# First batch of an attention and ReGLU kernel rebuilt: loads on 128 partitions, 64x64 transposes, one array tiling, operations picked by priority

## The chip, the cores and the metric

The kernel runs on one core of a Trainium2 chip. The metric is device time in microseconds (us), lower is better. "Fast" runs agree within about 1.5%; a run far above is "slow" and is left out of comparisons. Ratios are the mean time of one kernel's fast runs over the mean of the other's fast runs of the same rounds, so they are not quite the ratio of the medians that are quoted.

TensorE (PE) multiplies. Here it works as one 128x128 array (one matmul of 192 columns every 82 ns in the kernel before) or in 64x64 tiles, four of which run together; part of batch 0 ran in 128x64 tiles before. VectorE (DVE) and ScalarE (ACT) take results out of PSUM here. GpSimd (POOL) issues the loads, which cast float32 to bfloat16 on the way: 48.76 MB were read from HBM and 24.38 MB written by their queue. So the GB/s of the profile count the bytes written to the core's memory.

## The reference

```python
q, k, v: (8, 12, 448, 64)            # batch, heads, tokens, head size
scores = q @ k.T / sqrt(64)
attn   = maximum(scores, 0) ** 2 / 448
x      = (attn @ v) transposed to (3584, 768)
gate, val = maximum(x @ w_gate, 0), x @ w_val     # (768, 1536) each
out    = (gate * val) @ w_out                     # (1536, 768)
```

A batch is 448 tokens. Batch 0 has a schedule of its own, since nothing can be overlapped with its loads; later batches interleave the attention of one batch with the feed-forward part (FFN) of the batch before.

## The kernel before

A planner in Python gives every operation a start time from assumed durations and load rates, and the instructions are emitted in that order. TensorE ran strictly in it: matched by the name of what they write, none of the 8,414 matmuls of the kernel before starts more than 4 places from its place in the program. Batch 0 is split into two groups of its token columns, 192 and 256, so that the FFN of the first group can start early.

```python
def PARTS(b):
    return [(0, 192), (192, S - 192)] if b == 0 else [(0, S)]
...
# transposes: one head's q on partitions 0-63, its k on 64-127, 14 matmuls of 128 columns a head pair
nc.tensor.transpose(t_ps[64 * h2:64 * h2 + 64, i * 128:(i + 1) * 128],
                    st.qk[:, 4 * g + 2 * j + h2, t, :], ident)
...
class Product:                       # one output tile of 128 rows of the FFN
    def piece(self, row, k):
        if row is None:              # whole array: ONE matmul for 128 rows of the sum
            nc.tensor.matmul(self.out(), lhsT=self.weights(p, k), rhs=self.moving(p, k), ...)
            return
        p = slice(64 * row, 64 * row + 64)
        for col in range(2):         # 64x64 tiles: FOUR matmuls for the same work (2 rows x 2 columns)
            c = slice(64 * col, 64 * col + 64)
            ins = nc.tensor.matmul(self.out()[c], lhsT=self.weights(p, k)[:, c], rhs=self.moving(p, k), ...)
...
def chain_ops(prods):  ...           # 64x64: upper and lower half of the sum run staggered
def full_ops(prods):   ...           # 128x128
...
# batch 0 on the whole array, the rest in 64x64 tiles
ffn = full_ops([x for x in prods if x.b == 0]) + chain_ops([x for x in prods if x.b > 0])
```

Each matmul comes with a load of its weights, so a piece is 2 TensorE instructions on the whole array and 8 in 64x64 tiles. On the whole array a piece takes about columns/2400 us (82 ns were measured at 192 columns, 109 at 256), and four 64x64 matmuls side by side take the same.

Of the kernel before, what the change touches and what calls it, by code (L numbers as in the profile page):

```python
# [47 lines left out]
class Planner:  # L48
    LAT = 0.26
    NOUT = 8  # L50
    SWITCH = 0.095

# [37 lines left out]
    def commit(self, op, s, e):  # L90
        op.start, op.eng = s, e
# [25 lines left out]
def plan(att, ffn, others, pool, nburst, calm):  # L117
# [3 lines left out]
    P = Planner()  # L121
    ai = fi = pi = 0
# [4 lines left out]
    while ai < len(att) or fi < len(ffn) or pend or pi < len(pool):  # L127
# [12 lines left out]
        A = P.best(att[ai][0]) if ai < len(att) else None  # L140
        F = P.best(ffn[fi][1]) if fi < len(ffn) else None
        pick = None
        if A is not None and F is not None:
            if att[ai][1] == last_burst:
                pick = "A" if A[0] <= F[0] + 0.3 else "F"
            elif since >= gap:
                pick = "A" if A[0] <= F[0] + 0.1 else "F"
            else:
                pick = "F" if F[0] <= A[0] + 0.1 else "A"
        elif A is not None:  # L150
            pick = "A"
        elif F is not None:
            pick = "F"
        if pick == "A":
            cands.append((A[0], 2, A[2], 2, "PE", att[ai][0]))
# [7 lines left out]
        elif kind == 1:  # L163
            pend.remove(op)
        elif pick == "A":
# [22 lines left out]
def kernel(  # L188
# [100 lines left out]


    def PARTS(b):
        return [(0, 192), (192, S - 192)] if b == 0 else [(0, S)]
# [6 lines left out]
    def load_heads(b, h0, n, what="kv"):  # L299
        if b not in bat:  # L300
            bat[b] = Batch()
            bat[b].buf = Buf(r_in, NT if b >= XBAR_FROM else HP)
# [11 lines left out]
        rows = lambda x: x[b, hs].rearrange("h (p t) d -> p h t d", t=NT)  # L314
        rate = (240.0 if h0 == 4 else 290.0) if b == 0 else 340.0
        if "k" in what:
            k_op = dma_in(lambda: tile_of("qk", NT)[64:128, hs], rows(k), 64 * n, 112 * n, rate=rate, alloc=[st.buf] if h0 == 0 else [])
            q_op = dma_in(lambda: tile_of("qk", NT)[0:64, hs], rows(q), 64 * n, 112 * n, rate=rate)
            for h in range(h0, h0 + n):
                st.qk_op[h] = (k_op, q_op)  # L320
        if "v" in what:
            v0 = dma_in(lambda: tile_of("vv", NC + 2)[0:64, hs, 1:NC + 2], rows(v)[:, :, 0:NC + 1], 64 * n, 64 * n,
                        alloc=[st.vbuf] if h0 == 0 else [], rate=340.0)
            v1 = dma_in(lambda: tile_of("vv", NC + 2)[64:128, hs, 0:NC + 1], rows(v)[:, :, NC:NT], 64 * n, 64 * n, rate=340.0)
            for h in range(h0, h0 + n):
                st.v_op[h] = (v0, v1)
# [3 lines left out]
    def slot_order(b):  # L330
        return SIG if b % 2 == 0 else [SIG[-1]] + SIG[:-1]

# [7 lines left out]
    def columns_of(b):  # L340
        st = bat[b]
        if not hasattr(st, "qkT"):
            st.qkT = tpool.tile([128, 2, HP, S], BF16, name="qkT")
# [12 lines left out]
    def idle(n):  # L356
        for _ in range(n):
            nc.tensor.matmul(bank("w_ps"), lhsT=zeros[:, :128], rhs=zeros, start=True, stop=True)

    def transpose_pair(b, g, j):  # L360
# [3 lines left out]
        box = {}  # L364

        def emit():
            t_ps = box["t"] = bank("t_ps", BF16)
            for i, t in enumerate(slot_order(b)):
                for h2 in range(2):
                    nc.tensor.transpose(t_ps[64 * h2:64 * h2 + 64, i * 128:(i + 1) * 128],  # L370
                                        st.qk[:, 4 * g + 2 * j + h2, t, :], ident)

        def emit_copy():
            dst = columns_of(b)[:, :, 2 * g + j, :].rearrange("p a (t c) -> p t a c", c=P2)
            src = box["t"][:, :2 * S].rearrange("p (t a c) -> p t a c", t=NT, a=2)
            if cp.eng == "ACT":
                nc.scalar.copy(dst, src)
            else:
                nc.vector.tensor_copy(dst, src)  # L379

        h = 4 * g + 2 * j
        op = Op({"PE": 0.5 if g or b else 0.95}, emit, mode="C", deps=list(st.qk_op[h]) + list(st.qk_op[h + 1]) + [id_op],
                alloc=[ps], reads=[st.buf])
# [586 lines left out]
```

## Time and profile before

| | before |
|---|---|
| time | 434.10 us, median of 4 runs, one of 726 us included (the three others: 431.43 to 435.44, median 432.75) |
| span of the profiled run | 431.6 us |
| products alone, columns/2400 summed over the trace | 385.3 us |
| products done from 20 to 70 us, by the same sum | 36.6 us |
| TensorE instructions | 16,828 |

The first lines are of the page of the kernel before. The rows of digits show the busy share in 40 slices of the span (9 is 90% or more), PEclk the granted clock in tenths. "q8" is a DMA queue of kind "instruction": packets, MB and share of the DMA engines. The last line is the summary of the chain of waits.

```profile
span 431.6 us, 18155 instructions
PE 418.6 (97%) x8414; PEld 364.2 (84%) x8414; DVE 185.5 (43%) x346; ACT 241.8 (56%) x363; POOL 46.3 (11%) x72
PE   6699999999999999999999999999999999999995
PEclk9689999999999999999999999999999999999999
DMA  7999999894089946948865993790003200040014
q8 instruction: 66, 1.08, 1.0%
PE 92%; DMA 4%; POOL 1%; issue 0%; ACT 0%; SPq 0%; DVE 0%; POOLq 0%
```

TensorE is the limit. The DMA engines are full until about 70 us, and later only in some stretches.

The stretches from 25 to 70 us of the same run: busy time of each engine in the stretch with the number of its instructions, then clock, DMA share and GB/s.

```profile
core 0: us, PE busy (x) PEld busy (x) DVE busy (x) ACT busy (x) POOL busy (x), PEclk, DMA share, GB/s
25.00:40.00 15.00, 14.98 (x238) 11.36 (x235) 11.66 (x23) 12.05 (x23) 6.87 (x10) 1.00 1.40 199
40.00:55.00 15.00, 15.00 (x166) 10.86 (x164) 9.05 (x20) 10.59 (x17) 5.74 (x8) 1.00 1.39 201
55.00:70.00 15.00, 15.00 (x184) 10.53 (x183) 7.99 (x17) 9.44 (x17) 1.49 (x2) 1.00 1.30 203
```

TensorE never waits there (588 matmuls in 45 us). What it loses there is mostly extra time at changes of tiling. Three lines of the timeline, with start and duration in us:

```profile
37.11 0.67 PE L632 MATMUL g_ps<-xT,wg 128*128 128x192 bf16 x6
37.70 0.38 PE L494 MATMUL s_ps<-qkT 64*64 64x448 bf16 x4
38.02 0.67 PE L632 MATMUL v_ps<-xT,wv 128*128 128x192 bf16 x6
```

Matmuls of 192 columns follow each other every 82 ns, but the first one after a change of tiling ends 189 ns after the one before it. There are 70 such changes from 25 to 100 us, 7.9 us in all.

### The profile page before, as it was taken

The page shows a single profiled execution, that of the slowest core. Times are in us where ns is not written, and L with a number is a line of the kernel's source. Part 1 is how long each engine was busy: PE and PEld are TensorE (multiplying, and loading weights), DVE is VectorE, ACT ScalarE, POOL GpSimd, SP SyncE. Part 2 cuts the span into 40 slices and gives each one's busy share as a digit, 9 for nine tenths or more (in the row PEclk, how much of TensorE's full clock was granted, in tenths as well). Part 3 has the DMA queues.
Part 4 walks back from the last instruction along what each step waited for, and adds up shares of the span by engine and source line. Part 5 has one row for each costly group of instructions (what it writes and reads, how often), then busy time and mean ns, then how long its engine had stood idle before and what let it go on. Part 6 is the DMA issues. An engine that isn't in the chain of part 4 may idle for free.

```text
span 431.6 us, 18155 instructions
## 1 busy us (share of the span) xinstructions
PE 418.6 (97%) x8414; PEld 364.2 (84%) x8414; DVE 185.5 (43%) x346; ACT 241.8 (56%) x363; POOL 46.3 (11%) x72
## 2 busy tenths in 40 slices
PE   6699999999999999999999999999999999999995
PEld 2477776566688999899998999999998999999984
DVE  3776645224741665444435436533434434102200
ACT  2487666445766876664547656774547645332221
POOL 8536210010002002000200110010000000000000
PEclk9689999999999999999999999999999999999999
DMA  7999999894089946948865993790003200040014
GB/s 100 192 198 199 202 203 176 129 162 80 12 122 171 183 66 71 192 119 116 128 93 100 168 175 43 103 185 32 3 3 77 76 2 4 3 112 3 4 44 107
DMA packets 75213, 44.83 MB, mean 104 GB/s; under 512 B 34560, under 2 KB 71680, under 8 KB 75136
## 3 DMA queue, kind: packets, MB, share of 16 engines
q0 software_dynamic: 37856, 24.38, 39.8%
q1 hardware_dynamic: 37200, 19.17, 24.1%
q8 instruction: 66, 1.08, 1.0%
q10 hardware_dynamic: 80, 0.10, 0.1%
q14 instruction: 11, 0.09, 0.1%
HBM read 48.76 MB, written 11.01 MB: 138 GB/s over the span
## 4 chain that ended last, share of the span: by engine, by line
PE 92%; DMA 4%; POOL 1%; issue 0%; ACT 0%; SPq 0%; DVE 0%; POOLq 0%
PE o_ps L642 23%; PE v_ps L642 22%; PE g_ps L642 22%; PE s_ps L494 7%; PE s_ps L550 6%; PE v_ps L632 4%; PE g_ps L632 3%; DMA qkT<-spare 2%; PE o_ps L632 2%; DMA qk<-in_q_dram 2%; PE s_ps L501 1%; PE x_ps L575 1%; PE t_ps L370 1%; POOL qk L265 1%; POOL vv L265 0%
## 5 line engine op out<-in xcount | busy, mean ns | idle before, releaser
L511 ACT ACTIVATE r_sb<-s_ps 128x896 bf16<-128x896 f32 (+4 forms) x169 | 150.2, 895 | 73.4 <-PE s_ps L494 58.8
L642 PE MATMUL g_ps<-xT,wg 64*64 64x448 bf16 x2016 | 183.6, 349 | 0.3 <-ACT xT L596 0.3
L642 PE MATMUL v_ps<-xT,wv 64*64 64x448 bf16 x2016 | 176.5, 349 | 0.0
L529 DVE TENSOR_TENSOR at<-r_sb 128x896 bf16<-128x896 bf16 (+4 forms) x163 | 99.7, 616 | 99.8 <-ACT r_sb L511 99.6
L642 PE MATMUL o_ps<-wo,hT 64*64 64x384 bf16 x2400 | 126.0, 323 | 0.4 <-issue 0.4
L642 PEld LDWEIGHTS <-wg 64*64 64x64 bf16 x2016 | 113.1, 107 | 5.4 <-issue 0.5
L642 PEld LDWEIGHTS <-wv 64*64 64x64 bf16 x2016 | 113.0, 107 | 5.3
L642 PEld LDWEIGHTS <-hT 64*64 64x64 bf16 x2400 | 101.4, 107 | 12.1 <-issue 1.2
L732 DVE TENSOR_TENSOR hT<-v_ps,g_sb 128x448 bf16<-128x448 f32 (+2 forms) x108 | 61.8, 572 | 111.8 <-PE v_ps L642 97.9
L725 ACT ACTIVATE g_sb<-g_ps 128x448 bf16<-128x448 f32 (+2 forms) x107 | 53.7, 502 | 57.8 <-PE g_ps L642 46.7
L494 PE MATMUL s_ps<-qkT 64*64 64x448 bf16 (+2 forms) x648 | 66.8, 341 | 2.4 <-DVE qkT L379 1.1
L777 ACT ACTIVATE o_sb<-o_ps 128x384 f32<-128x384 f32 (+1 forms) x55 | 27.2, 494 | 31.1 <-PE o_ps L642 22.5
L494 PEld LDWEIGHTS <-qkT 64*64 64x64 bf16 x648 | 30.9, 109 | 10.9 <-issue 6.1
L550 PE MATMUL s_ps<-at,vv 64*64 64x448 bf16 x588 | 39.6, 350 | 0.0
L596 ACT CAST xT<-s_ps 128x896 bf16<-128x896 f32 (+1 forms) x22 | 19.6, 892 | 20.6 <-PE s_ps L550 20.0
L550 PEld LDWEIGHTS <-vv 64*64 64x64 bf16 x612 | 26.8, 108 | 4.2 <-issue 1.8
L265 POOL DMA_DIRECT2D vv<-in_v_dram x22 | 15.5, 717 | 42.5 <-PE s_ps L550 32.8
L847 POOL COPY mark<-qkT 64x1 bf16<-64x1 bf16 x5 | 1.0, 198 | 175.8 <-DMA qkT<-spare 175.8
L632 PE MATMUL v_ps<-xT,wv 128*128 128x192 bf16 (+1 forms) x144 | 17.9, 261 | 0.0
L632 PE MATMUL g_ps<-xT,wg 128*128 128x192 bf16 (+1 forms) x144 | 17.8, 260 | 0.0
L632 PEld LDWEIGHTS <-wv 128*128 128x128 bf16 x144 | 11.6, 98 | 4.7 <-issue 4.0
L632 PEld LDWEIGHTS <-wg 128*128 128x128 bf16 x144 | 12.9, 98 | 1.5 <-issue 0.6
(36 smaller groups left out, 134.0 us busy)
## 6 DMA issues: line engine op xcount, KB each, us to landing
out_dram<-o_sb SPq DMA_DIRECT2D x54, 192.0 KB, 3.2
vv<-in_v_dram POOLq DMA_DIRECT2D x12, 384.0 KB, 12.5
qk<-in_k_dram POOLq DMA_DIRECT2D x6, 672.0 KB, 7.3
qk<-in_q_dram POOLq DMA_DIRECT2D x6, 672.0 KB, 10.8
wg<-in_moe_w_gate_dram POOLq DMA_DIRECT2D x6, 384.0 KB, 11.2
wv<-in_moe_w_val_dram POOLq DMA_DIRECT2D x6, 384.0 KB, 11.4
wo<-in_moe_w_out_dram POOLq DMA_DIRECT2D x2, 1152.0 KB, 17.2
qk<-in_k_dram POOLq DMA_DIRECT2D x5, 224.0 KB, 10.6
```

The source lines that it names most:

```text
L265: op = Op({"POOL": 0.58 + 0.0004 * n_desc}, lambda: nc.gpsimd.dma_start(out=dst(), in_=src), deps=deps, alloc=alloc, xfer=kb / rate)
L370: nc.tensor.transpose(t_ps[64 * h2:64 * h2 + 64, i * 128:(i + 1) * 128], st.qk[:, 4 * g + 2 * j + h2, t, :], ident)
L494: nc.tensor.matmul(half_of(h2)[o:o + P2, m * n:(m + 1) * n], lhsT=kq(1, j, h2, key_off(b) + c * 128 + o, P2), rhs=kq(0, j, h2, self.c0, n) ...
L511: nc.scalar.activation(dst, src, AF.Relu)
L529: lambda: nc.vector.tensor_tensor(self.at_tile(i), loc["r"][:, :2 * ne], loc["r"][:, :2 * ne], ALU.mult),
L550: ins = nc.tensor.matmul(x_of(slice(64 * h2, 64 * h2 + 64), j), lhsT=st.vv[p, 4 * g + 2 * j + h2, (NC + 1) * (1 - row) if tail else 1 + c, :],
L596: nc.scalar.copy(dst, src)
L632: nc.tensor.matmul(self.out(), lhsT=self.weights(p, k), rhs=self.moving(p, k), start=(k == 0), stop=(k == self.nk - 1))
L642: ins = nc.tensor.matmul(self.out()[c], lhsT=self.weights(p, k)[:, c], rhs=self.moving(p, k), start=(row == 0 and k == 0), stop=(row == 1 ...
L725: nc.scalar.activation(loc["gs"], gp.out(), AF.Relu)
L732: nc.vector.tensor_tensor(hs["hT"][:, mf, t0:t0 + n], vp.out(), loc["gs"], ALU.mult)
L777: nc.scalar.activation(out=dst, in_=src, func=AF.Copy, scale=float(out_scale))
```

## The change

Its intent: batch 0 no longer changes the tiling, the loads of keys and queries of batches 0 and 1 reach all partitions, and the head of the kernel takes whatever is ready. In core, with cuts marked:

```diff
 def PARTS(b):
-    return [(0, 192), (192, S - 192)] if b == 0 else [(0, S)]
+    return [((NT - QA) * P2, QA * P2), (0, (NT - QA) * P2)] if b == 0 else [(0, S)]     # QA = 3: again 192 and 256
 ...
 # loads of batches 0 and 1: two heads side by side on 128 partitions, queries of batch 0 in two pieces (a, b)
+    pt = lambda x: x[b, hs].rearrange("(a c) (p t) d -> (c p) a t d", c=2, t=NT)
+    LOADS = ("k0002 a0002 k0404 a0404 I k0202 a0804 a0202 v0004 k0804 b0012 v0408 g0 g1 g2 kqv1004 g3 "
+             "kqv1804 kqv1404 g4 g5 o0 o1")
 ...
 # transposes: 28 matmuls of 64 columns a head pair, in the two diagonal 64x64 tiles
+    nc.tensor.transpose(t_ps[p, (m * n + i) * 64:(m * n + i + 1) * 64], qk[p, w, hp, t, :], ident[p, p])
 ...
 # batch 0's product with v: the 64x64 form of the other batches
-    if not self.full:
-        xo, op = None, whole
 ...
 # FFN of batch 0: first six of twelve row tiles in two parts, the others with all 448 columns
-    order += [(p, m) for m in range(n1, KF) for p in (pa, pb)]
+    ... + [((0, S), m) for m in range(n1, KF)]
 ...
-    ffn = full_ops([x for x in prods if x.b == 0]) + chain_ops([x for x in prods if x.b > 0])
+    ffn = chain_ops(prods)
 ...
 # planner: head operations by priority; dummy matmuls fill planned gaps of the head
+    soon = min(b[0] for b, _ in first) + P.SOON
+    A, now = next(x for x in first if x[0][0] <= soon)
+    filler = (r_f, 0.216, lambda n: Op({"PE": 0.216 * n}, lambda: idle(n), mode="F"))
```

More of the change, by code (lines that the diff above doesn't have):

```diff
@@ L51 @@
     SWITCH = 0.095
+    SOON = 0.02
+    AHEAD = 0.1
     def __init__(self):
@@ L90, in commit @@
     def commit(self, op, s, e):
+        if e == "PE" and self.filler and 3.0 <= self.t.get(e, 0.0) < 24.0:
+            res, one, make = self.filler
+            t = max(self.t[e], min(res.free, default=1e9) + self.LAT)
+            n = int((s - t - 0.35) / one)
+            if n > 0:
+                fill = make(n)
+                self.mode = fill.mode
+                fill.start, fill.eng, fill.end = t, e, t + n * one
+                res.free.remove(min(res.free))
+                res.free.append(fill.end)
+                self.t[e] = fill.end
+                self.ops.append(fill)
         op.start, op.eng = s, e
@@ L114, in commit, with plan @@
         self.ops.append(op)
-def plan(att, ffn, others, pool, nburst, calm):
+def plan(head, att, ffn, others, pool, nburst, calm, filler):
     P = Planner()
+    P.filler = filler
     ai = fi = pi = 0
@@ L126, in plan @@
     gap = 0.0
-    while ai < len(att) or fi < len(ffn) or pend or pi < len(pool):
+    while head or ai < len(att) or fi < len(ffn) or pend or pi < len(pool):
         cands = []
@@ L139, in plan @@
                 cands.append((s, 0, 0.0, 0, "POOL", pool[pi]))
-        A = P.best(att[ai][0]) if ai < len(att) else None
+        A = P.best(att[ai][0]) if ai < len(att) and not head else None
+        first = [(b, op) for b, op in ((P.best(op), op) for op in head) if b is not None]
+        if first:
+            soon = min(b[0] for b, _ in first) + P.SOON
+            A, now = next(x for x in first if x[0][0] <= soon)
         F = P.best(ffn[fi][1]) if fi < len(ffn) else None
@@ L143, in plan @@
         if A is not None and F is not None:
-            if att[ai][1] == last_burst:
+            if head:
+                pick = "A" if A[0] <= F[0] + P.AHEAD else "F"
+            elif att[ai][1] == last_burst:
                 pick = "A" if A[0] <= F[0] + 0.3 else "F"
@@ L154, in plan @@
         if pick == "A":
-            cands.append((A[0], 2, A[2], 2, "PE", att[ai][0]))
+            cands.append((A[0], 2, A[2], 2, "PE", now if head else att[ai][0]))
         elif pick == "F":
@@ L164, in plan @@
             pend.remove(op)
+        elif pick == "A" and head:
+            head.remove(op)
         elif pick == "A":
@@ L287 @@
     SIG = [x for j in range(NC) for x in (j, NC + 1 + j)] + [NC]
+    QA = 3
     def PARTS(b):
-        return [(0, 192), (192, S - 192)] if b == 0 else [(0, S)]
+        return [((NT - QA) * P2, QA * P2), (0, (NT - QA) * P2)] if b == 0 else [(0, S)]
     class Batch:
@@ L301, in load_heads @@
             bat[b] = Batch()
-            bat[b].buf = Buf(r_in, NT if b >= XBAR_FROM else HP)
+            bat[b].buf = Buf(r_in, NT if b >= XBAR_FROM else HP + (NQ if b == 0 else 0))
             bat[b].vbuf = Buf(r_v, NQ * len(PARTS(b)))
@@ L313, in load_heads @@
         hs = slice(h0, h0 + n)
-        rows = lambda x: x[b, hs].rearrange("h (p t) d -> p h t d", t=NT)
-        rate = (240.0 if h0 == 4 else 290.0) if b == 0 else 340.0
-        if "k" in what:
-            k_op = dma_in(lambda: tile_of("qk", NT)[64:128, hs], rows(k), 64 * n, 112 * n, rate=rate, alloc=[st.buf] if h0 == 0 else [])
-            q_op = dma_in(lambda: tile_of("qk", NT)[0:64, hs], rows(q), 64 * n, 112 * n, rate=rate)
-            for h in range(h0, h0 + n):
-                st.qk_op[h] = (k_op, q_op)
@@ L321, in load_heads @@
-        if "v" in what:
-            v0 = dma_in(lambda: tile_of("vv", NC + 2)[0:64, hs, 1:NC + 2], rows(v)[:, :, 0:NC + 1], 64 * n, 64 * n,
-                        alloc=[st.vbuf] if h0 == 0 else [], rate=340.0)
-            v1 = dma_in(lambda: tile_of("vv", NC + 2)[64:128, hs, 0:NC + 1], rows(v)[:, :, NC:NT], 64 * n, 64 * n, rate=340.0)
-            for h in range(h0, h0 + n):
-                st.v_op[h] = (v0, v1)
+        if b < XBAR_FROM:
+            pt = lambda x: x[b, hs].rearrange("(a c) (p t) d -> (c p) a t d", c=2, t=NT)
+            dst = lambda w, t0, t1: tile_of("qk", NT).rearrange("p (w a) t d -> p w a t d", w=2)[:, w, h0 // 2:(h0 + n) // 2, t0:t1]
+            for c, x, w, t0, t1 in (("k", k, 1, 0, NT), ("q", q, 0, 0, NT), ("a", q, 0, 0, QA), ("b", q, 0, QA, NT)):
+                if c in what:
+                    op = dma_in(lambda w=w, t0=t0, t1=t1: dst(w, t0, t1), pt(x)[:, :, t0:t1], 64 * n, 16 * (t1 - t0) * n,
+                                alloc=[st.buf] if h0 == 0 and c == "k" else [])
+                    for h in range(h0, h0 + n):
+                        st.qk_op[(c if c != "q" else "a", h)] = op
+        else:
+            rows = lambda x: x[b, hs].rearrange("h (p t) d -> p h t d", t=NT)
+            if "k" in what:
+                k_op = dma_in(lambda: tile_of("qk", NT)[64:128, hs], rows(k), 64 * n, 112 * n, rate=340.0,
+                              alloc=[st.buf] if h0 == 0 else [])
+                q_op = dma_in(lambda: tile_of("qk", NT)[0:64, hs], rows(q), 64 * n, 112 * n, rate=340.0)
+                st.qk_op[0] = (k_op, q_op)
@@ L330, in slot_order, with q_order @@
+        if "v" in what:
+            for r in range(2):
+                src = v[b, hs].rearrange("h (p t) d -> p h t d", t=NT)[:, :, NC * r:NC * r + NC + 1]
+                op = dma_in(lambda r=r: tile_of("vv", NC + 1)[64 * r:64 * r + 64, hs], src, 64 * n, 64 * n,
+                            alloc=[st.vbuf] if h0 == 0 and r == 0 else [], rate=340.0)
+                for h in range(h0, h0 + n):
+                    st.v_op.setdefault(h, []).append(op)
     def slot_order(b):
         return SIG if b % 2 == 0 else [SIG[-1]] + SIG[:-1]
+    def q_order(b):
+        return slot_order(b) if b else list(range(QA, NT)) + list(range(QA))
@@ L342, in columns_of @@
         if not hasattr(st, "qkT"):
-            st.qkT = tpool.tile([128, 2, HP, S], BF16, name="qkT")
+            t = tpool.tile([128, 2 * HP * S], BF16, name="qkT")
+            st.flat = t
+            st.qkT = t.rearrange("p (a w s) -> p w a s" if b < XBAR_FROM else "p (w a s) -> p w a s", w=2, s=S)
         return st.qkT
@@ L356, in idle, with turn @@
     def idle(n):
+        w_ps = bank("w_ps")
         for _ in range(n):
-            nc.tensor.matmul(bank("w_ps"), lhsT=zeros[:, :128], rhs=zeros, start=True, stop=True)
-    def transpose_pair(b, g, j):
+            nc.tensor.matmul(w_ps, lhsT=zeros[:, :128], rhs=zeros, start=True, stop=True)
+    def turn(b, hps, what):
         st = bat[b]
@@ L364, in transpose_pair @@
         box = {}
+        qs = q_order(b)
+        if b:
+            todo = [(0, t) for t in qs]
+        else:
+            todo = [(0, t) for t in (qs[NT - QA:] if what == "a" else qs[:NT - QA])]
+        if what == "a":
+            todo += [(1, t) for t in slot_order(b)]
+        n = len(todo)
+        c0 = (NT - QA) * P2 if what == "a" and b == 0 else 0
         def emit():
             t_ps = box["t"] = bank("t_ps", BF16)
-            for i, t in enumerate(slot_order(b)):
-                for h2 in range(2):
-                    nc.tensor.transpose(t_ps[64 * h2:64 * h2 + 64, i * 128:(i + 1) * 128],
-                                        st.qk[:, 4 * g + 2 * j + h2, t, :], ident)
+            qk = st.qk.rearrange("p (w a) t d -> p w a t d", w=2)
+            for m, hp in enumerate(hps):
+                for i, (w, t) in enumerate(todo):
+                    for h2 in range(2):
+                        p = slice(64 * h2, 64 * h2 + 64)
+                        nc.tensor.transpose(t_ps[p, (m * n + i) * 64:(m * n + i + 1) * 64], qk[p, w, hp, t, :], ident[p, p])
         def emit_copy():
-            dst = columns_of(b)[:, :, 2 * g + j, :].rearrange("p a (t c) -> p t a c", c=P2)
-            src = box["t"][:, :2 * S].rearrange("p (t a c) -> p t a c", t=NT, a=2)
+            columns_of(b)
+            dst = st.flat.rearrange("p (a x) -> p a x", a=HP)[:, hps[0]:hps[-1] + 1, c0:c0 + n * 64]
+            src = box["t"][:, :len(hps) * n * 64].rearrange("p (a x) -> p a x", a=len(hps))
             if cp.eng == "ACT":
@@ L379, in emit_copy @@
                 nc.vector.tensor_copy(dst, src)
-        h = 4 * g + 2 * j
-        op = Op({"PE": 0.5 if g or b else 0.95}, emit, mode="C", deps=list(st.qk_op[h]) + list(st.qk_op[h + 1]) + [id_op],
-                alloc=[ps], reads=[st.buf])
-        cp = Op({"DVE": 0.57, "ACT": 0.84}, emit_copy, deps=[op], alloc=[st.tbuf] if g == 0 and j == 0 else [],
-                reads=[ps], prio=0, bias=0.0)
+        kinds = ("a", "k") if what == "a" else ("b",)
+        deps = list({id(o): o for o in (st.qk_op[(c, 2 * hp + h2)] for hp in hps for c in kinds for h2 in range(2))}.values())
+        cols = 64 * n * len(hps)
+        op = Op({"PE": 0.1 + 0.056 * n * len(hps)}, emit, mode="Q", deps=deps + [id_op], alloc=[ps], reads=[st.buf])
+        cp = Op({"DVE": 0.125 + cols / 1920.0, "ACT": 0.11 + cols / 1200.0}, emit_copy, deps=[op],
+                alloc=[st.tbuf] if what == "a" and hps[0] == 0 else [], reads=[ps], prio=0, bias=0.0)
         others.append(cp)
-        t_op[(b, 2 * g + j)] = cp
+        for hp in hps:
+            t_op.setdefault((b, hp), []).append(cp)
         return op
@@ L421, in transpose_batch @@
         for hp in range(HP):
-            t_op[(b, hp)] = xo[1]
+            t_op[(b, hp)] = [xo[1]]
         return xo
@@ L443, in __init__, with turned @@
             self.box, self.at_buf, self.base = shared or ({}, Buf(r_pair if home else r_at, 1), 0)
+        def turned(self, hp):
+            ops = t_op[(self.b, hp)]
+            assert self.c0 or self.full or len(ops) == 2
+            return ops[:1] if self.c0 else ops
         def size(self):
@@ L454, in at @@
             t, n = self.box["at"], self.n
-            i = NC * j + c if self.full else c
+            i, m = (NC * j + c, 0) if self.full else divmod(NC * j + c, 2)
             w = 1 if self.full else 2
-            o = self.base + (2 * i + h2) * w * n + (0 if self.full else j * n)
+            o = self.base + (2 * i + h2) * w * n + m * n
             return t[:, o:o + n]
@@ L474, in s @@
             ps = [Buf(r_f, 1), Buf(r_f, 1)] if single else [Buf(r_s, 1)]
-            js = [i // NC] if self.full and not tail else [0, 1]
-            c = i % NC
+            places = [divmod(i, NC)] if self.full else [divmod(2 * i, NC), divmod(2 * i + 1, NC)]
+            js = [0, 1] if tail else sorted({j for j, _ in places})
             ne = n if tail or self.full else 2 * n
@@ L490, in emit @@
                 if not tail:
-                    for m, j in enumerate(js):
+                    for m, (j, c) in enumerate(places):
                         for h2 in range(2):
@@ L503, in emit @@
                                              rhs=kq(0, j, h2, self.c0, n), start=True, stop=True)
-            op = Op({"PE": (0.01 if self.full else 0.04) + ne / 2400.0}, emit, mode="Q", deps=[t_op[(b, 2 * g + j)] for j in js],
+            op = Op({"PE": (0.01 if self.full else 0.04) + ne / 2400.0}, emit, mode="Q", deps=[d for j in js for d in self.turned(2 * g + j)],
                     alloc=ps + ([self.at_buf] if i == 0 and self.own else []), reads=[st.tbuf])
@@ L551, in fours @@
                                 x_of(slice(64 * h2, 64 * h2 + 64), j),
-                                lhsT=st.vv[p, 4 * g + 2 * j + h2, (NC + 1) * (1 - row) if tail else 1 + c, :],
+                                lhsT=st.vv[p, 4 * g + 2 * j + h2, NC * (1 - row) if tail else c + row, :],
                                 rhs=(self.at_tail(h2) if tail else self.at(j, c, h2))[p],
@@ L565, in pv @@
             dv = [d for h in range(4 * g, 4 * g + 4) for d in st.v_op[h]]
-            def emit_xy():
-                loc["x"] = [bank("x1_ps"), bank("x1_ps")] if split else bank_pair()
-                fours([NC], 0)
-                for j in range(2):
-                    for c in range(NC):
-                        for h2 in range(2):
-                            o = slice(64 * h2, 64 * h2 + 64)
-                            dst = loc["x"][j][o, :n] if split else loc["x"][o, j, :n]
-                            nc.tensor.matmul(dst, lhsT=st.vv[:, 4 * g + 2 * j + h2, 1 + c, :], rhs=self.at(j, c, h2),
-                                             start=False, stop=(c == NC - 1), skip_group_check=True)
-            whole = Op({"PE": 0.11 + (2 * NC + 1) * (n / 2400.0 + 0.003)}, emit_xy, mode="QC", deps=self.sq + dv, alloc=ps,
-                       reads=[self.at_buf, st.vbuf])
             xo = Op({"PE": 0.02 + (NC + 1) * (n / 2400.0 + 0.003)}, emit_x, mode="Q", deps=self.sq + dv, alloc=ps)
@@ L602, in pv @@
                 if first:
-                    st.x_buf = Buf(r_x, 2 * KF * len(PARTS(b)))
+                    st.x_buf = Buf(r_x, 2 * KF + (KF if len(PARTS(b)) == 2 else 0))
                 cp = Op(on_psum(n if split else 2 * n), None, deps=[op], alloc=[st.x_buf] if first else [], reads=[ps[j]],
@@ L717, in product @@
             return Product(name, b, n, KD, lambda p, kd: w[c][p, kd, o:o + 128], lambda p, kd: st.xT[p, kd, cols],
-                           deps=xop[(b, c0)] + [dep], reads=[st.x_buf])
+                           deps=(xop[(b, c0)] if n < S or b else xop[(0, PARTS(0)[0][0])] + xop[(0, 0)]) + [dep], reads=[st.x_buf])
         gp, vp = product("g_ps", w_gate_sb, wg_op[c]), product("v_ps", w_val_sb, wv_op[c])
@@ L750, in ffn_prods @@
             n1 = KF // 2
-            order = [(pa, m) for m in range(n1)] + [(pb, m) for m in range(n1)]
-            order += [(p, m) for m in range(n1, KF) for p in (pa, pb)]
+            order = [(pa, m) for m in range(n1)] + [(pb, m) for m in range(n1)] + [((0, S), m) for m in range(n1, KF)]
         else:
@@ L803, in emit_store @@
                         if ti < NC:
-                            dst = rows(b0)[SIG[2 * ti + half]]
+                            dst = rows(b0)[q_order(b0)[2 * ti + half]]
                         elif ti == NC:
-                            dst = rows(b0 + half)[SIG[-1]]
+                            dst = rows(b0 + half)[(q_order(b0)[-1], SIG[-1])[half]]
                         else:
@@ L821, in ffn_prods @@
         return res
-    load_heads(0, 0, 2, "k")
-    load_heads(0, 2, 2, "k")
-    id_op = Op({"POOL": 0.35}, identity)
-    pool_ops.append(id_op)
-    load_heads(0, 4, 4, "k")
-    load_heads(0, 0, 4, "v")
-    load_heads(0, 8, 4, "k")
-    load_heads(0, 4, 8, "v")
-    load_gv(0)
-    load_gv(1)
-    load_gv(2)
-    load_heads(1, 0, 4)
-    load_gv(3)
-    load_heads(1, 4, 4)
-    load_gv(4)
-    load_gv(5)
-    load_out(0)
-    load_heads(1, 8, 4)
-    load_out(1)
+    LOADS = ("k0002 a0002 k0404 a0404 I k0202 a0804 a0202 v0004 k0804 b0012 v0408 g0 g1 g2 kqv1004 g3 "
+             "kqv1804 kqv1404 g4 g5 o0 o1")
+    for x in LOADS.split():
+        if x == "I":
+            id_op = Op({"POOL": 0.35}, identity)
+            pool_ops.append(id_op)
+        elif x[0] == "g":
+            load_gv(int(x[1]))
+        elif x[0] == "o":
+            load_out(int(x[1]))
+        else:
+            load_heads(int(x[-4]), int(x[-3], 16), int(x[-2:]), x[:-4])
     mark = const.tile([P2, 1], BF16)
@@ L869, in T @@
             for j in range(2):
-                att.append((transpose_pair(b, g, j), nb))
+                att.append((turn(b, [2 * g + j], "a"), nb))
     (ca, na), (cb, nbc) = PARTS(0)
@@ L875 @@
     Bp = [Part(0, g, cb, nbc, A[g].share()) for g in range(NQ)]
-    def W(n, us):
-        if n:
-            att.append((Op({"PE": us}, lambda: idle(n), mode="F", alloc=[Buf(r_f, 1)]), nb))
-            att[-1][0].reads = att[-1][0].alloc
     def first_zeros():
@@ L884, in first_zeros @@
         idle(8)
-    att.append((Op({"PE": 3.0}, first_zeros, mode="F"), nb))
-    ORDER = ("T0 W2 T1 A0:0f A0:1 W2 A0:3 W2 A0:2 T2 T3 A1:0 A1:1f A1:3 T4 T5 A1:2 A2:0 A2:1f A2:2 VA0f A2:3 "
-             "B0:0 VA1f B0:3 VA2f B0:1f B0:2 / B1:0 B2:0 VB0f / / B2:1f / B1:2 B2:3 B1:3 B1:1 / / B2:2 VB1f VB2")
-    for x in ORDER.split():
-        part = {"A": A, "B": Bp}
-        single = x[-1] == "f"
-        if x == "/":
-            nb += 1
-        elif x[0] == "T":
-            att.append((transpose_pair(0, int(x[1]) // 2, int(x[1]) % 2), nb))
-        elif x[0] == "W":
-            W(int(x[1]), 0.25 * int(x[1]))
-        elif x[0] == "V":
-            att.append((part[x[1]][int(x[2])].pv(single)[1], nb))
-        else:
-            att.append((part[x[0]][int(x[1])].s(int(x[3]), single), nb))
+    head = {"W": Op({"PE": 3.0}, first_zeros, mode="F")}
+    ORDER = ("W B03 YA0 A00 T3 XA1f T2 A13 A03 B10f U0 B00 XA2f A23f YB1 A22f A20f U2 T5 A21 A10 B23 "
+             "A11f XB0 A12 XB2 XA0 B13 A02 YA1 T0 T4 YA2 B02f B01 B21f B11 B12 B20 XB1 B22 U1 T1 YB0 "
+             "A01f YB2")
+    names = ORDER.split()
+    for x in range(HP):
+        head["T%d" % x] = turn(0, [x], "a")
+    for x in range(NQ):
+        head["U%d" % x] = turn(0, [2 * x, 2 * x + 1], "b")
+    for p, parts in (("A", A), ("B", Bp)):
+        for g, part in enumerate(parts):
+            for i in range(NC + 1):
+                name = "%s%d%d" % (p, g, i)
+                head[name] = part.s(i, name + "f" in names)
+            name = "%s%d" % (p, g)
+            head["X" + name], head["Y" + name] = part.pv("X" + name + "f" in names)
+    head = [head[x.rstrip("f")] for x in names]
     prev = Bp[2]
@@ L931 @@
     prods = [x for b in range(B) for x in ffn_prods(b)]
-    ffn = full_ops([x for x in prods if x.b == 0]) + chain_ops([x for x in prods if x.b > 0])
+    ffn = chain_ops(prods)
     def nburst(b, cur):
         return xburst[b + 1] - cur + 1 if b + 1 < B else 0
-    for op in plan(att, ffn, others, pool_ops, nburst, calm):
+    filler = (r_f, 0.216, lambda n: Op({"PE": 0.216 * n}, lambda: idle(n), mode="F"))
+    for op in plan(head, att, ffn, others, pool_ops, nburst, calm, filler):
         op.emit()
```

## The prediction

> **What bounds the kernel now.** TensorE. The page has PE busy 97% of a 431.6 us span; the chain of waits puts 92% on PE. The trace's matmuls at columns/2400 us each (the pace of back-to-back ones; a quarter for 64x64 tiles, as four run together) add up to 385.3 us that no order avoids. The other 46 us, by stretch:
>
> - 0 to 25 us: 21.3 us lost. The DMA list shows batch 0 landing until 18.3 us and the first gate weights at 19.9. The windows show 137 to 147 GB/s from 6 to 12 us, 197 to 200 from 14; the clock is halved from 14.8 to 25.0 us. The first FFN product starts at 25.7 us.
> - 25 to 100 us: 13.9 us lost. The timeline shows 70 changes of array tiling (128x128, 128x64, 64x64), each 0.11 us over a normal step: 7.9 us. Batch 1's transposes take 2.6 us.
> - 100 to 420 us: 5.4 us, 1.6%: this code's floor. The last 12 us lose 6.1 in the drain.
>
> **What the change does.**
> 1. Everything runs in 64x64 tiling. Nearly all 70 changes go: -7.5 us, on the critical path, since PE hardly waits there. [...] Products of 192 columns still take 82 ns a step in 64x64 (scores of before), so narrow ones lose nothing.
> 2. Transposes become 28 of 64 columns a head pair, not 14 of 128. Before, two took 56 ns (0.43 us a pair). The change books 56 ns for each diagonal couple, 0.8 us a pair: +2.4 us in batch 1; batch 0's falls in idle time.
> 3. Loads fill 128 partitions, keys first, 4/7 of the queries deferred. [...] With 200 GB/s from 6 us, batch 0 is in by about 15 us, the first gate weights by 16.5.
> 4. Priority picking and dummy matmuls in gaps let part A of the attention finish near 17 us and keep the clock full. FFN starts near 17.5 us, not 25.7, with as much attention done: -8 us. ACT and DVE limit attention (about 33 us of work together for batch 0), so perhaps 1.5 us is given back up to 28 us.
> 5. Later, loads can starve the faster PE: the output weights land near 61 us (64.5 before). I book 1 us.
>
> Sum: -7.5 +2.4 -8 +1.5 +1, about -12 us on the span; measured time is about 2 us above it.
>
> **Prediction:** 421 us, range 414 to 428. Chances: faster by over 2% 0.74, within 2% 0.24, slower 0.02.
>
> **What would show it.** 1: no 128x128 matmuls beyond the dummies; the 75 us after the FFN's start lose 6 to 7 us, not 14. 2: 0.8 us a pair. 3: 190 GB/s from 6 us, batch 0 landed by 15. 4: first gate matmul at 16 to 19 us, no half clock after 5 us. From 120 us: unchanged.
>
> **What would make it wrong.** Loads no faster at the head (768-byte query pieces), so that FFN starts near 21; landings in another order than planned, so that PE, strictly in order, stalls and its clock halves; ACT and DVE setting the pace up to 40 us; starvation at the output weights or batch 2.

As written the terms come to -10.6 us, where the text says about -12. The 200 GB/s from 6 us in point 3, and with it most of the -8 us of point 4, was the author's estimate: the trace before shows 137 to 147 GB/s from 6 to 12 us and 194 to 199 from 14 to 18 us, but not why. That dummies keep the clock full was also an estimate from that trace: the clock was full while dummies ran, the last at 9.9 us, and halved from 14.8 us.

## The result, and the profile after

The change made the kernel slower: 449.01 us (median of 4 runs, 448.36 to 449.66) against 434.10, ratio 1.0365, 95% interval 1.0301 to 1.0428. The predicted 421 us, with 0.74 for faster, was wrong in its direction.

The page of the kernel after, the same lines:

```profile
span 448.0 us, 20188 instructions
PE 416.6 (93%) x9449; PEld 331.1 (74%) x9449; DVE 185.0 (41%) x342; ACT 240.7 (54%) x357; POOL 48.0 (11%) x73
PE   7766669999999989999999999998999999999995
PEclk9698899999999999999999999999999999999998
DMA  8999999069709991796669399499001300040014
q8 instruction: 74, 1.21, 1.1%
PE 81%; DMA 9%; issue 4%; POOL 2%; SPq 1%; DVE 1%; ACT 1%; POOLq 0%
```

TensorE is now 60 to 70% busy in slices 3 to 6, about 22 to 67 us, where it was 90% or more. Of the whole span, 4% of the chain is "issue": waiting for nothing that the profile shows. The stretches from 25 to 70 us:

```profile
core 0: us, PE busy (x) PEld busy (x) DVE busy (x) ACT busy (x) POOL busy (x), PEclk, DMA share, GB/s
25.00:40.00 15.00, 9.45 (x328) 8.98 (x324) 7.67 (x16) 6.72 (x11) 7.25 (x11) 0.89 1.40 199
40.00:55.00 15.00, 9.87 (x300) 9.28 (x303) 4.50 (x9) 4.90 (x9) 8.06 (x10) 0.89 1.41 199
55.00:70.00 15.00, 10.64 (x279) 8.93 (x275) 5.90 (x11) 6.30 (x10) 0.00 (x0) 0.89 1.32 205
```

It issued 907 matmuls in these 45 us, half as many again, but did less: products of 23.1 us from 20 to 70 us against 36.6 before. DVE and ACT are emptier too; POOL, which issues the loads, is slightly fuller in two of the stretches. The largest waits of TensorE from 20 to 70 us, with total us, times and the longest:

```profile
PE v_ps L684 <- issue: 7.8, 4, 3.1
PE g_ps L684 <- issue: 6.7, 3, 2.9
PE x_ps L608 <- issue: 1.1, 1, 1.1
```

Two of them in the timeline of TensorE. The bracket gives idle time and what ended it:

```profile
26.43 0.38 PE L552 MATMUL s_ps<-qkT 64*64 64x256 bf16 x8
26.64 0.25 PE L684 MATMUL v_ps<-xT,wv 64*64 64x192 bf16 x4
28.98 0.43 PE L684 MATMUL v_ps<-xT,wv 64*64 64x192 bf16 x10 [2.09 <-issue]
...
31.81 0.25 PE L684 MATMUL v_ps<-xT,wv 64*64 64x192 bf16 x2
35.18 0.85 PE L684 MATMUL v_ps<-xT,wv 64*64 64x192 bf16 x14 [3.12 <-issue]
```

The stalled matmul at 28.98 us is the middle of a product that already runs: its weights and data are there, and it waits for no semaphore. What it has in common with the others showed when the matmuls of the trace were laid beside the program's list of TensorE instructions. The stalls of over 0.5 us between 21 and 67 us fall on instructions number 704, 960, 1216, 1472, 1728, 1984, 2240 and 2496: exactly 256 apart. Together they are 17.1 us (from start to start, less the usual step; the view above counts 15.6 us of it as idle). The "instruction" queue fits: 18,898 TensorE instructions in blocks of 256 are 74 blocks, and 74 packets are what it moved, 16,384 bytes each (64 bytes an instruction); before, 16,828 are 66. Between 20 and 67 us these packets start at 20.4, 26.5, 32.7, 38.9, 45.1, 51.3, 57.4 and 63.3 us: one each 5.9 to 6.2 us. Each starts 3.7 us after TensorE entered the block before it, and TensorE goes on 6.2 us after that entry. So in this stretch the blocks come one at a time, and where TensorE uses up 256 instructions in less than 6.2 us, it waits for the rest. In the kernel before, a block lasted 8.3 to 12.1 us in the same stretch.

Why blocks last less long now: 256 instructions are 128 matmuls. On the whole array at 192 columns these are about 10.5 us of work (128 times 82 ns). As four tiles they are 32 steps of 82 ns, 2.6 us; at 448 columns, 32 steps of 189 ns, 6.05 us.

The clock also fell near waits: the clock records show half clock from 34.7 to 38.1, 48.4 to 51.8 and 65.4 to 68.9 us, 3.41 us each. The longest waits near the three were 3.1, 2.9 and 2.0 us; after others, of 2.1 us at 29.0 and 59.7 us, the clock stayed full.

### The profile page after: what moved, and what is told of

Same layout as the page of the kernel before. It is cut to its first block, busy times and chain, and to the rows that moved or that the text cites. A ratio compares the mean times of both kernels' runs of the same rounds, so it can differ in the third digit from the quotient of the medians.

```text
span 448.0 us, 20188 instructions
## 1 busy us (share of the span) xinstructions
PE 416.6 (93%) x9449; PEld 331.1 (74%) x9449; DVE 185.0 (41%) x342; ACT 240.7 (54%) x357; POOL 48.0 (11%) x73
## 4 chain that ended last, share of the span: by engine, by line
PE 81%; DMA 9%; issue 4%; POOL 2%; SPq 1%; DVE 1%; ACT 1%; POOLq 0%
PE v_ps L684 23%; PE g_ps L684 23%; PE o_ps L684 22%; PE s_ps L608 6%; PE s_ps L552 6%; DMA qkT<-spare 4%; DMA vv<-in_v_dram 4%; DMA qk<-in_q_dram 2%; POOL qk L288 1%; SPq L464 1%; PE s_ps L559 1%; PE t_ps L421 1%; POOL vv L288 0%; PE x_ps L608 0%; DVE qkT L430 0%
## 5 line engine op out<-in xcount | busy, mean ns | idle before, releaser
L684 PE MATMUL g_ps<-xT,wg 64*64 64x448 bf16 (+2 forms) x2448 | 213.4, 342 | 7.2 <-issue 6.7
L684 PE MATMUL v_ps<-xT,wv 64*64 64x448 bf16 (+2 forms) x2448 | 206.2, 342 | 9.7 <-issue 9.4
L684 PEld LDWEIGHTS <-wg 64*64 64x64 bf16 x2448 | 122.0, 109 | 35.0 <-issue 8.0
L684 PE MATMUL o_ps<-wo,hT 64*64 64x384 bf16 x2688 | 143.4, 323 | 0.0
L587 DVE TENSOR_TENSOR at<-r_sb 128x896 bf16<-128x896 bf16 (+2 forms) x163 | 99.7, 617 | 97.4 <-ACT r_sb L569 96.8
L684 PEld LDWEIGHTS <-hT 64*64 64x64 bf16 x2688 | 115.0, 107 | 10.8 <-issue 0.4
L552 PE MATMUL s_ps<-qkT 64*64 64x448 bf16 (+2 forms) x648 | 72.9, 342 | 1.4 <-DMA qkT<-spare 1.1
L608 PE MATMUL s_ps<-at,vv 64*64 64x448 bf16 (+2 forms) x672 | 47.1, 342 | 1.6 <-DMA vv<-in_v_dram 1.6
L638 ACT CAST xT<-s_ps 128x896 bf16<-128x896 f32 (+2 forms) x25 | 21.3, 851 | 26.6 <-PE s_ps L608 26.6
L559 PE MATMUL s_ps<-qkT 64*64 64x448 bf16 (+2 forms) x108 | 13.9, 344 | 0.2 <-ACT r_sb L569 0.2
L454 DVE COPY spare<-qk 128x768 bf16<-128x768 bf16 x42 | 12.4, 352 | 0.0
```

What stands on the lines that cost most here:

```text
L552: nc.tensor.matmul(half_of(h2)[o:o + P2, m * n:(m + 1) * n], lhsT=kq(1, j, h2, key_off(b) + c * 128 + o, P2), rhs=kq(0, j, h2, self.c0, n) ...
L559: nc.tensor.matmul(half_of(h2)[64 * j:64 * j + 64, :n], lhsT=kq(1, j, h2, key_tail(b), P2), rhs=kq(0, j, h2, self.c0, n), start=True, stop ...
L587: lambda: nc.vector.tensor_tensor(self.at_tile(i), loc["r"][:, :2 * ne], loc["r"][:, :2 * ne], ALU.mult),
L608: ins = nc.tensor.matmul(x_of(slice(64 * h2, 64 * h2 + 64), j), lhsT=st.vv[p, 4 * g + 2 * j + h2, NC * (1 - row) if tail else c + row, :], ...
L638: nc.scalar.copy(dst, src)
```

## The experiments

Theory F: under full loads the fetch brings 256 TensorE instructions per 6.2 us, and 64x64 tiling of narrow products needs more. Rival L: the new order of loads (all of batch 1's heads ahead of the last weights; gate weights 4 and 5 land at 48.4 and 52.4 us, before at 43.4 and 47.3) starves TensorE. A later rival P: the planner expects loads too early, and TensorE, which runs strictly in the planned order, then waits for data (3.7 us for batch 0's queries and keys in the changed kernel).

### One part undone: batch 0's FFN on the whole array again

```diff
-    ffn = chain_ops(prods)
+    ffn = full_ops([x for x in prods if x.b == 0]) + chain_ops([x for x in prods if x.b > 0])
```

> The changed kernel with one part undone: batch 0's feed-forward products run on the whole 128x128 array again, a quarter of the TensorE instructions for the same columns. Theory F (instruction fetch: while the loads fill the DMA engines, 256 TensorE instructions arrive per 6.2 us and no faster): the eight stalls of 1.3 to 3.4 us at every 256th instruction between 21 and 67 us go or fall under 0.5 us each, the clock is not halved after 30 us, and the time falls by about 15 us, to 430 to 437, below or near before. Theory L (order of loads: all of batch 1's heads now land ahead of the last weights, which come 5 us later than before): the loads are the same, so TensorE still starves and the time stays at 444 to 450.

Measured: 430.90 us (before in the same rounds 432.48), ratio 0.9960 (0.9924 to 0.9997). Stretches from 25 to 70 us, and the only wait of TensorE of kind "issue" from 20 to 70 us:

```profile
25.00:40.00 15.00, 14.84 (x280) 11.18 (x280) 10.09 (x21) 9.61 (x19) 6.69 (x10) 1.00 1.40 199
40.00:55.00 15.00, 15.00 (x171) 9.01 (x168) 8.67 (x17) 10.24 (x16) 8.58 (x11) 1.00 1.40 199
55.00:70.00 15.00, 15.00 (x164) 6.76 (x164) 7.43 (x13) 8.39 (x12) 0.00 (x0) 1.00 1.32 203
...
PE x_ps L608 <- issue: 0.4, 1, 0.4
```

The loads are as full as in the changed kernel (199 to 203 GB/s against 199 to 205), but the stalls are gone, and with them 18 us. One line of the change is its whole loss; all the rest of it together is worth 0.4%. By the sum of products, about 13 of the 18 us lie between 25 and 100 us and 5 between 100 and 420 us, where later waits of the changed kernel (named below) go too; so the 18 us are not the eight stalls alone, though they come near to their sum. One stall of 0.56 us stays, at instruction 704 again, in batch 0's attention.

### That part alone, in the kernel before

```diff
-    ffn = full_ops([x for x in prods if x.b == 0]) + chain_ops([x for x in prods if x.b > 0])
+    ffn = chain_ops(prods)
```

> The kernel before with one part of the change alone: batch 0's feed-forward products in 64x64 tiling, its loads and head as they were. Theory F: stalls appear at every 256th TensorE instruction from about 26 to 70 us, chunks of 256 take 6.2 us each, and the time rises by 10 us or more, to 443 or above, although about 30 changes of tiling into and out of 128x128 go. Theory L: the loads are those of before, so nothing starves, and the time falls by 3 to 6 us.

Measured: 447.61 us, ratio 1.0356 (1.0319 to 1.0394). Stretches and waits as above:

```profile
25.00:40.00 15.00, 9.39 (x321) 7.37 (x310) 7.85 (x18) 6.97 (x14) 6.41 (x10) 1.00 1.39 199
40.00:55.00 15.00, 13.27 (x365) 11.99 (x365) 8.53 (x18) 7.08 (x10) 6.24 (x9) 0.89 1.39 201
55.00:70.00 15.00, 8.59 (x291) 7.54 (x280) 6.17 (x12) 7.91 (x13) 1.49 (x2) 1.00 1.33 202
...
PE g_ps L642 <- issue: 6.0, 3, 2.3
PE v_ps L642 <- issue: 2.0, 2, 1.1
```

With the old loads in the old order the loss appears in full, so L is not needed for it. TensorE also waits 2.6 us for ACT here, since the planned order no longer fits, and the stalls go on to the end of the loads: 3.0 us at 68 and 1.3 us at 76 us.

### The order of loads put back

```diff
-    LOADS = ("... v0408 g0 g1 g2 kqv1004 g3 "
-             "kqv1804 kqv1404 g4 g5 o0 o1")
+    LOADS = ("... v0408 g0 g1 g2 g3 kqv1004 "
+             "g4 g5 kqv1404 o0 kqv1804 o1")
```

> The changed kernel with the loads of batch 1's heads moved behind the gate and value weights, near the order of before. Theory F: the DMA engines are as full and the instructions as many, so chunks still take 6.2 us between 23 and 66 us and the time stays within 444 to 453. Theory L: the weights land 5 us earlier, the stalls go, and the time falls to 440 or below.

Measured: 445.69 us, ratio to before 1.0313 (1.0273 to 1.0354). TensorE's largest waits from 20 to 70 us:

```profile
PE v_ps L684 <- issue: 4.4, 2, 2.3
PE t_ps L421 <- issue: 4.0, 2, 2.3
PE g_ps L684 <- issue: 3.7, 2, 3.1
```

The stalls stay, on the same instruction numbers. The order of loads is worth 2 to 3 us here, not the loss.

### The same narrow products where the DMA engines are idle

The last batch's gate and value products are cut into 256 and 192 columns too. (Two bookkeeping lines, not shown: the number of readers, and which part of x a product waits for.)

```diff
-            order = [(PARTS(b)[0], m) for m in range(KF)]
+            order = [(p, m) for m in range(KF) for p in (PARTS(0) if b == B - 1 else PARTS(b))]
```

> The changed kernel with the last batch's gate and value products also cut into 256 and 192 columns, so that 256 TensorE instructions hold only 2.6 to 3.5 us of work there, at a time (about 360 to 410 us) when the DMA engines are nearly idle. Theory F with saturation as the cause of the slow fetch: no or small stalls at every 256th instruction there (under 0.5 us each), and 447 to 453 us in all. Theory F with a fetch that is slow in itself (6 us, loads or not): every chunk there takes about 6 us, so 17 to 20 us more, 465 us or above. Theory L says nothing of it, and expects no change.

Measured: 454.81 us, median of 4 runs of which one was slow (459.1), ratio to before 1.0486 (1.0422 to 1.0550), about 5 us above the change. The profile is of the slow run; in the stretch in question it is undisturbed. Two stretches of it, and the largest wait from 403 to 438 us:

```profile
410.00:420.00 10.00, 8.70 (x338) 8.04 (x332) 2.45 (x7) 2.53 (x7) 0.00 (x0) 1.00 0.02 5
420.00:430.00 10.00, 9.02 (x348) 8.30 (x339) 3.13 (x8) 2.48 (x7) 0.00 (x0) 1.00 0.02 4
...
PE g_ps L684 <- issue: 2.2, 5, 0.6
```

From 407 to 434 us blocks of narrow instructions took 3.7 to 4.0 us here, with small stalls at every 256th instruction (0.3 to 0.6 us idle); the packet starts 1.0 to 1.7 us after the entry. So the fetch took a time of its own here, 3.7 to 4.0 us, and both versions of F held a part. That full loads make 6.2 us of it is tested next. The 64x64 form of narrow products is not slow in itself.

### The same instructions, with loads that nobody reads

Nothing is added to the kernel just shown but a gate and 14 loads, from the end of the last batch's first product on. The list of TensorE instructions is the same, one by one.

```diff
+    def again(i):
+        if i % 2 == 0:
+            extra["t"] = inp.tile([128, H, NT, D], BF16, name="qk")
+        x = (k, q)[i % 2]
+        nc.gpsimd.dma_start(out=extra["t"][64 * (1 - i % 2):64 * (1 - i % 2) + 64],
+                            in_=x[i // 2].rearrange("h (p t) d -> p h t d", t=NT))
+    for i in range(14):
+        pool_ops.append(Op({"POOL": 0.9}, lambda i=i: again(i), deps=[first], xfer=3.4))
```

> The kernel with a narrow last batch, its TensorE instructions unchanged one by one, and nothing added but 14 loads of 672 KB into buffers that nobody reads, started when the last batch's first product is done (about 405 us). In the run without them, 256 narrow instructions took 3.7 to 4.1 us there, with the DMA engines nearly idle. If full DMA engines are what slows the fetch: chunks of 256 take about 6.2 us while the loads run, with stalls of 2 us or more at every 256th instruction, and the time rises by 10 to 18 us, to 463 to 472. If the fetch takes the same time under any load: 452 to 456, as without the loads.

Measured: 474.81 us, median of 4 runs of which one was slow (480.4), ratio to before 1.0954 (1.0858 to 1.1049). Stretches, and the large waits from 403 to 456 us:

```profile
410.00:420.00 10.00, 4.40 (x154) 4.18 (x157) 1.31 (x4) 1.05 (x3) 1.50 (x2) 0.93 1.27 206
420.00:430.00 10.00, 7.23 (x238) 6.73 (x231) 2.24 (x6) 1.81 (x5) 1.83 (x3) 0.90 1.27 206
...
PE g_ps L684 <- issue: 11.6, 5, 2.8
PE v_ps L684 <- issue: 4.1, 2, 2.9
```

Loads that no instruction waits for cost 20 us. Block by block, in the two runs (worked out from the trace and the list of instructions):

| stretch | 256 instructions take | packet starts after entry of the block before |
|---|---|---|
| before, 23 to 75 us | 8.3 to 12.1 us | 1.2 to 2.4 us |
| after, 23 to 66 us | 5.9 to 6.2 us | 3.7 us |
| narrow last batch, 404 to 438 us | 3.5 to 4.2 us | 1.0 to 1.7 us |
| the same with 14 loads, 406 to 455 us | 5.9 to 6.5 us | 3.6 to 4.2 us |

This shows the cause: with the same TensorE instructions, full loads stretch a fetch from 3.7 to 4.0 us to about 6 (5.9 to 6.5). That both pass through DMA queues is in the profile; at which point of that path the fetch waits is not shown. The first row is a warning: the loads were as full there, yet the packet started 1.2 to 2.4 us after the entry and not 3.7. TensorE did not stall there; why the packet came earlier is not shown. The time was 3 us above the expected range; the granted clock, 0.90 to 0.93 in the rows, may account for it.

### The planner told slower loads, all in 64x64

```diff
-    ... rate=380.0):                                   # default, weights and heads
+    ... rate=366.0):
-    ... 1536, 2160)                                    # output weights
+    ... 1536, 2160, rate=335.0)
-    alloc=[st.buf] if h0 == 0 and c == "k" else [])    # keys and queries of batches 0, 1
+    alloc=[st.buf] if h0 == 0 and c == "k" else [], rate=300.0 if b == 0 else 380.0)
-    ... rate=340.0)                                    # v
+    ... rate=300.0 if b == 0 else 340.0)
-    reads=[pair], xfer=1.0)                            # DMA transpose
+    reads=[pair], xfer=2.5)
```

> The changed kernel, all in 64x64, with nothing but the planner's rates corrected as above. Theory P (a rival: TensorE runs strictly in order, and a plan that expects loads 1 to 4 us too early makes it wait for data): the stalls go and the time falls by 10 us or more, to 439 or below. Theory F: the instructions still arrive 256 per 6.2 us, so 444 to 450.

Measured: 447.34 us, ratio 1.0340 (1.0290 to 1.0389); the profiled run was an outlier of 1111 us and is not read. The time lies in the range of F, so P is not the cause.

### Four versions in search of a faster one

The first keeps only batch 0's narrow products on the whole array; its 448-column and output products stay in 64x64 tiles.

```diff
-    ffn = chain_ops(prods)
+    ffn = full_ops([x for x in prods if x.b == 0 and x.n < S and x.nk == KD]) + chain_ops(
+        [x for x in prods if x.b > 0 or x.n == S or x.nk > KD])
```

> The changed kernel, with only the narrow (192 and 256 columns) products of batch 0 on the whole array; its 448-column and output products stay in 64x64. Theory F reckons 256 instructions of 448 columns as 6.05 us of work against 6.2 us for a fetch under full loads, so wide products should cost almost nothing extra and save changes of tiling from about 40 us on: stalls only at transposes, under 0.7 us each, and a time of 427 to 432. If instead any 64x64 work under full loads is slow, it lands at 435 to 441, between the version with all of batch 0 on the whole array (430.9) and the change (449.0).

Measured: 435.35 us, ratio 1.0103 (1.0044 to 1.0161). That is a miss for F; it falls just inside the other range, but not for its reason: from 50 to 60 us the kernel did 9.9 us of products in 10, so wide 64x64 products under full loads are not slow as such. It lost 2.1 us at 90 us, waiting for batch 2's transposed keys, which it reached earlier, and 1.9 us at a block boundary at 287 us, where the last batch's loads moved 202 GB/s. So wide products (6.05 us a block against a fetch of 6.2) are at the edge where such loads run, not free.

The second has all of batch 0 on the whole array and 300 GB/s in the planner for batch 0's loads.

```diff
-    ffn = chain_ops(prods)
+    ffn = full_ops([x for x in prods if x.b == 0]) + chain_ops([x for x in prods if x.b > 0])
-    ... (keys, queries and v of batch 0: 380 and 340 GB/s)
+    ... (300 GB/s)
```

> All of batch 0's products on the whole array, and the planner told 300 GB/s in place of 380 and 340 for batch 0's loads, since they landed 1.6 to 2.3 us later than planned and the clock was halved for 6.8 us in the head. If the plan's early landings keep the head from gaining: dummies fill the waits of 8 to 16 us, no half clock in the head, and 2 to 4 us less than the 430.9 of the version without it. If the loads alone set the head: first feed-forward product still at 24 to 25 us and 429 to 432.

Measured: 430.13 us, ratio 0.9972 (0.9943 to 1.0002). The first FFN product moved from 26.0 to 23.9 us and the half clock shrank from 6.8 to 3.4 us, but the total was 0.8 us below the first experiment's, whose rounds were others, and the ratio is no better (0.9972 against 0.9960): no gain is shown.

The third has the whole array for batch 0 and the weights ahead of batch 1's heads (both diffs above).

> All of batch 0's products on the whole array, and batch 1's heads behind the weights. With the fetch stalls gone, the order of loads may show for itself: theory L's remnant expects 2 to 4 us less than 430.9; theory F expects no difference, 429 to 432.

Measured: 434.72 us, ratio 1.0079 (1.0047 to 1.0110): a miss for both; once nothing stalls on instructions, the change's own order of loads is the better one by 4 to 5 us.

The fourth has narrow products on the whole array and 300 GB/s in the planner.

> Both of the above parts together: narrow products of batch 0 on the whole array, and the planner told 300 GB/s for batch 0's loads. If both help and add up: 425 to 429. If the head is set by the loads: equal to the version with the narrow products alone.

Measured: 432.84 us, ratio 1.0033 (1.0009 to 1.0058); neither expectation holds, it is 2.5 us better than the narrow products alone, yet no better than before.

Two more have all of the planner's rates as in the run above: one with the narrow products, one with all of batch 0 on the whole array.

> Narrow products of batch 0 on the whole array, the rest in 64x64, and the planner told the rates and the transpose latency that the traces show (300 GB/s for batch 0, 366 for gate and value weights, 335 for output weights, 1.5 us more for a DMA transpose). If the 1.1 to 2.1 us wait for batch 2's transposed keys near 91 us came from the plan's early landing, it goes: 428 to 431. If the loads set it: 432 to 434, as without it (432.8).

Measured: 430.20 us, ratio 0.9961 (0.9928 to 0.9994), in the first range; one of its six runs, the profiled one, was an outlier of 1649 us, so its waits can't be read.

> All of batch 0's products on the whole array and the same measured rates in the planner. 428 to 431, faster than before by 0.3 to 0.8%, if each part helps; equal to 430.1 (only batch 0's rates corrected) if the rest of the rates do not matter.

Measured: 432.47 us, ratio 1.0014 (0.9983 to 1.0045), a miss and no gain. The best versions are the narrow products with these rates (0.9961) and the first experiment (0.9960). They beat both kernels, but the one before by 0.4% only.

## Why the prediction was wrong

1. **"Nearly all 70 changes go: -7.5 us ... so narrow ones lose nothing" is the step that failed.** Its first half held: from 25 to 100 us no change of tiling is left, and from 70 to 100 us, when most of its loads are done, the time beyond products fell from 3.7 to 1.9 us. The second half held for the pace of matmuls (82 ns a step) but not for their supply. The sum counted columns and never instructions: the same columns take four times the instructions in 64x64 tiles, 2.6 us of work per block of 256 against a fetch of 6.2 us. The eight stalls sum to 17.1 us, and undoing this one line won 18 us in all.

2. **Transposes at 0.8 us a pair: mis-sized.** I took 56 ns a couple from the planner of the change. The trace shows 32 ns at full clock, 0.45 us a pair, against 0.39 before (7 couples of 56 ns). They cost next to nothing.

3. **Batch 0 landed by 15 us, gate weights by 16.5: failed.** They landed at 18.5 and 20.4 us, before at 18.3 and 19.9. The windows still show 143 to 160 GB/s from 6 to 14 us. That 128 partitions alone would bring 200 GB/s there was the author's estimate, and it was not shown. The prediction also overlooked that v's loads still go to 64 partitions at a time. The added loads that nobody reads, each to 64 partitions in turn, moved 206 GB/s, weights on 128 partitions 197 to 200, so no run here shows 64 partitions slower. What holds back the first 14 us was not settled; packets of 896 bytes took 101 ns on average from 6 to 14 us and 88 ns later, those of 384 bytes (the query pieces of 768 bytes, cast) 51 ns from 6 to 14 us, while POOL issued loads without a break (busy 8.00 of these 8 us).

4. **FFN from 17.5 us, no half clock: failed.** The first gate product started at 24.7 us (25.7 before), since its data came no earlier, and the clock was halved from 14.2 to 21.1 us: the planner had put dummies only into gaps that it expected, the last one at 11.3 us, and TensorE waited 1.3 us for keys until 13.3 us. This was in my list of what could go wrong. With the planner told the rates, the product came 2.1 us earlier, but no gain in all is shown. So the term of -8 us, the largest of the sum, came to 1.0 us in the changed kernel, taken as the earlier start of the FFN.

5. **Starvation at the output weights: not seen.** They landed at 66.8 us; TensorE was so late that it never asked for them earlier. "From 120 us: unchanged" was also off: the changed kernel waits there 1.8 us for v at 165, 1.3 us for transposed keys at 188, and 1.8 us at a block boundary at 307 us.

## What to carry to other kernels

Count instructions as well as columns: where loads fill the DMA engines, TensorE here got 256 instructions, that is 128 matmuls with their weight loads, per 6.2 us, so check that 128 matmuls last longer than that when splitting work into tiles (with narrow products of 2.6 us of work a block TensorE stalled for 17.1 us in all; before, at 8.3 to 12.1 us a block, it did not). Waits of kind "issue" on instructions without a semaphore, at even distances in the program (here eight, 256 instructions apart), pointed to the fetch of instructions; the "instruction" DMA queue shows its packets. Before a planned order is trusted, compare the planner's landing times with those of a trace.
